# Seven half-size products in place of eight for w_out in a gated MLP with linear attention, with one centring pass and a new order of steps

## The chip, the cores and the metric

The kernel runs on one core of one Trainium2 chip. The time is the core's device time for one execution, in microseconds (us), as a median of several runs. The engines are TensorE (PE, with its weight loads as PEld), VectorE (DVE), ScalarE (ACT), GpSimd (POOL) and the queue of SyncE (SP), which issues the loads and stores. Matmuls read SBUF and add up in PSUM.

## What is computed

Eight batches of linear attention (8 heads, 576 positions, 64 channels) feed a gated MLP whose gate mixes positions. Cut to what matters:

```python
q_s = softmax(q, axis=-1); k_s = softmax(k, axis=2)      # each with 1e-9 added to the sum
kv = np.einsum('bhsd,bhse->bhde', k_s, v)
x = np.einsum('bhsd,bhde->bhse', q_s, kv)                # -> (8, 576, 512)
h = gelu_tanh(x @ w_in)                                  # w_in 512 x 1024
u, v = h[..., :512], h[..., 512:]
v_n = (v - mean(v)) / np.sqrt(var(v) + 1e-06) * g_ln     # over the 512 channels
v_s = np.einsum('ts,bsd->btd', w_sg, v_n) + b_sg[None, :, None]   # w_sg 576 x 576
out = x + (u * v_s) @ w_out                              # w_out 512 x 512
```

## The kernel before

All is float32, and every dense product is made of numbers split in two: a high part rounded to the fast matmul format and a low part that holds the rest. A product is then three matmuls, high by high, high by low and low by high, added in PSUM. The low part is made by one subtraction, the high part by one cast.

The channels of a batch lie on the 128 partitions in blocks of 128, and the 576 positions along the row in two halves of 288. A batch goes through these steps, each a small function: the softmax of q and k (`q_max`, `q_sub`, `q_exp`, `q_sum`, `q_inv`, `q_mul`, and `k_...`, with copies between partition groups in `q_swapm`, `q_swapd`, `k_rota`, `k_rotb`), `kv_mm`, `xm_mm` (x and its two parts `xm_high`, `xm_low`), `hv_mm b i` (the v half of w_in for one block of 128 positions, 12 matmuls of 512 columns), `hu_mm b f` (the u half for one block of channels, 24 matmuls of 288 columns; batch 0 has it in pieces, `hu_part`), the norm (`hv_gelu`, `hv_sq` or the statistics in `hv_stat`, `hv_pow`, `hv_norm`, `hv_high`, `hv_low`, and `tail_...` for the last 64 positions), `sg_mm b d` (the product with w_sg, 28 matmuls of 288), `gate b d` (times u), `gate_high`, `gate_low`, `out_mm b e` (w_out, 24 matmuls of 288 for each of four blocks e, 96 a batch), `out_base` (x again, from its two parts), `out_add` (PSUM added to it) and `out_store`. In the last batch the last block is done in two halves (`last_mm`, `last_add`, `last_store`).

`hv_norm` takes the mean off and multiplies by g_ln in one pass on DVE; `hv_high` and `hv_low` apply 1/sqrt(var) as a scale while they make the two parts:

```python
V.scalar_tensor_tensor(out=t, in0=t, scalar=mean, in1=g_bc[n], op0=op, op1=ALU.mult)
A.activation(vn_h()[:, i], v_s(b, i), AF.Copy, scale=rs_s(b, i))
V.scalar_tensor_tensor(out=lo[:, i], in0=v_s(b, i), scalar=rs_s(b, i), in1=f32(hi[:, i]), op0=ALU.mult, op1=ALU.subtract)
```

The order of all this is written out by hand: the string `PLAN` names the steps one after the other, a letter behind a step choosing the engine (V, A, G for DVE, ACT, POOL). Each engine runs its own steps in the order of that string; `InOrder` (its helper `issue`, line 163 of the profile, L180 afterwards) binds DVE, ACT, POOL and SP to it, and `mm` (line 252, afterwards L283) binds PE. So steps of three or four batches are interleaved: while one batch is in its gate, the next ones are in their softmax and norm. Nothing overtakes on an engine.

PSUM has eight banks. Three pairs (`ps2`, names ps_0_77, ps_1_78, ps_2_79) turn round for the products whose result has two halves of 288, one bank for each half; two single banks (`ps1`, ps_0_80, ps_1_81) turn round for hv_mm and kv_mm. A tile that is filled again waits for what still reads it. The framework keeps waits by tile: for a pair of banks, a matmul into one half counts as touching the tile that DVE reads.

At the start the weights come as 64-bit numbers, are turned into floats by integer operations (`wi_a` to `wi_d`, `wo_a` to `wo_d`) and split. `warm n` is a pair of matmuls with the identity whose result nobody reads; there are eight of them, all before the first hu_part.

## Time and profile before

| | before |
|---|---|
| median of 3 runs | 495.14 us (494.0 to 495.35) |
| the profiled execution | 495.75 us, of which span 494.0 |
| PE busy | 480.7 us, 97% |
| DVE busy | 348.5 us, 71% |
| ACT busy | 285.6 us, 58% |
| POOL busy | 168.8 us, 34% |

The span is the time from the first to the last instruction that the profiler saw; the run's own time is 1.75 us longer. Matmuls overlap, so their mean duration (298 ns for 288 columns) is not the distance from one to the next; that is read from starts. Rows of groups give the number of instructions, then their busy time and the mean in ns, then the idle time before them. Rows of a timeline give the start, the duration, the engine, the line of the code and the operation with its tiles; "f32 x4" there is a merged run of four.

### The profile page before, as it was taken

The page shows a single profiled execution, that of the slowest core. Times are in us where ns is not written, and L with a number is a line of the kernel's source. Part 1 is how long each engine was busy: PE and PEld are TensorE (multiplying, and loading weights), DVE is VectorE, ACT ScalarE, POOL GpSimd, SP SyncE. Part 2 cuts the span into 40 slices and gives each one's busy share as a digit, 9 for nine tenths or more (in the row PEclk, how much of TensorE's full clock was granted, in tenths as well). Part 3 has the DMA queues.
Part 4 walks back from the last instruction along what each step waited for, and adds up shares of the span by engine and source line. Part 5 has one row for each costly group of instructions (what it writes and reads, how often), then busy time and mean ns, then how long its engine had stood idle before and what let it go on. Part 6 is the DMA issues. An engine that isn't in the chain of part 4 may idle for free.

```text
span 494.0 us, 9497 instructions
## 1 busy us (share of the span) xinstructions
PE 480.7 (97%) x3847; PEld 445.6 (90%) x3847; DVE 348.5 (71%) x611; ACT 285.6 (58%) x607; POOL 168.8 (34%) x133
## 2 busy tenths in 40 slices
...
DMA packets 16302, 47.51 MB, mean 96 GB/s; under 512 B 1922, under 2 KB 3332, under 8 KB 16260
## 3 DMA queue, kind: packets, MB, share of 16 engines
...
## 4 chain that ended last, share of the span: by engine, by line
PE 80%; DVE 9%; DMA 3%; ACT 3%; POOL 2%; issue 2%; SPq 0%; POOLq 0%
PE ps L252 80%; DMA raw_i_vnh<-w_in 1%; DVE v L163 1%; DMA vv<-v 1%; POOL qq L163 1%; DVE ot_i L163 1%; DVE ot_o L163 1%; POOL wi_l L163 1%; DVE km L163 1%; DVE o L163 1%; DMA eye<-identity 1%; DVE vnl L163 1%; ACT L163 1%; ACT kk L163 0%; DVE qt L163 0%
## 5 line engine op out<-in xcount | busy, mean ns | idle before, releaser
L163 POOL TENSOR_TENSOR ulow<-u,gh 128x576 fp32r<-128x576 f32 x21 | 33.4, 1593 | 90.0 <-ACT gh L163 48.5
L163 POOL TENSOR_TENSOR rs<-ve,half 128x1 f32<-128x1 f32 x36 | 26.2, 734 | 96.3 <-DVE ve L163 96.3
L252 PE MATMUL ps<-gh,wo_h 128*128 128x288 f32 x256 | 56.1, 298 | 0.0
L252 PE MATMUL ps<-ulow,wo_h 128*128 128x288 f32 x256 | 55.5, 296 | 0.0
L252 PE MATMUL ps<-gh,wo_l 128*128 128x288 f32 x256 | 55.4, 295 | 0.0
L252 PE MATMUL ps<-ws_h,vnh 128*128 128x288 f32 x256 | 55.2, 297 | 0.0
L163 DVE TENSOR_TENSOR u<-ps,u 128x576 f32<-128x576 f32 x32 | 23.8, 750 | 44.1 <-PE ps L252 39.0
L252 PE MATMUL ps<-ws_h,vnl 128*128 128x288 f32 x256 | 54.9, 296 | 0.0
L252 PE MATMUL ps<-ws_l,vnh 128*128 128x288 f32 x256 | 54.9, 296 | 0.0
L163 ACT ACT_TABLE_LOAD x34 | 43.6, 1283 | 2.7 <-issue 2.0
L163 ACT CAST gh<-u 128x576 fp32r<-128x576 f32 x32 | 20.8, 669 | 41.6 <-DVE u L163 41.5
L163 POOL TENSOR_TENSOR qq<-qq,qm 128x1152 f32<-128x1152 f32 (+2 forms) x10 | 20.9, 2092 | 67.5 <-DVE qm L163 26.8
L252 PEld LDWEIGHTS ps<-ws_h,vnh 128*128 128x128 f32 x256 | 41.4, 188 | 0.8
L252 PEld LDWEIGHTS ps<-gh,wo_h 128*128 128x128 f32 x256 | 41.3, 188 | 0.9 <-DVE x_l L163 0.2
L163 ACT ACTIVATE vnh<-v,rs 128x512 fp32r<-128x512 f32 x32 | 22.9, 723 | 33.0 <-DVE v L163 18.4
L252 PEld LDWEIGHTS ps<-gh,wo_l 128*128 128x128 f32 x256 | 41.3, 188 | 0.0
L252 PEld LDWEIGHTS ps<-ulow,wo_h 128*128 128x128 f32 x256 | 41.2, 188 | 0.0
L252 PEld LDWEIGHTS ps<-ws_h,vnl 128*128 128x128 f32 x256 | 41.1, 188 | 0.0
L252 PEld LDWEIGHTS ps<-ws_l,vnh 128*128 128x128 f32 x256 | 41.0, 188 | 0.0
L252 PE MATMUL ps<-x_h,wi_h 128*128 128x288 f32 (+2 forms) x256 | 40.6, 298 | 0.4 <-DVE o L163 0.3
L163 DVE TENSOR_TENSOR o<-ps,o 128x576 f32<-128x576 f32 (+1 forms) x33 | 24.0, 729 | 23.4 <-PE ps L252 20.5
L252 PE MATMUL ps<-wi_h,x_h 128*128 128x512 f32 x144 | 39.8, 397 | 0.4 <-ACT v L163 0.4
(128 smaller groups left out, 1116.5 us busy)
## 6 DMA issues: line engine op xcount, KB each, us to landing
...
out<-o SPq DMA_DIRECT2D x31, 288.0 KB, 2.7
...
ghws<-w_sg SPq DMA_DIRECT2D x5, 288.0 KB, 8.4
x_lk<-k_turn SPq DMA_DIRECT2D x4, 288.0 KB, 4.3
...
raw_i_vnh<-w_in SPq DMA_DIRECT2D x2, 512.0 KB, 7.4
```

Of the source, the lines that this page charges most:

```text
L163: ins = op(*args, **kw)
L252: tc.keep_in_program_order(nc.tensor.matmul(*args, **kw))
```

## The change

From batch 1 on (`FROM`) w_out is done by the scheme of Strassen and Winograd. The gated u (512 channels) and w_out (512 by 512) are cut in halves of 256 channels, u also in halves of 288 positions; seven products of half size (`out_p b t m`, m from 1 to 7, t for the two blocks of 128 output channels in a half, six matmuls each) replace the eight. Their operands are quarters of u and four sums of them, made in place (`t_1` to `t_4`) and split (`p_high`, `p_low`) into three slots each; the weights' sums are made once (`s1_a` to `s4_b`, `s_h`, `s_l`). The products of a t lie in the two banks of one PSUM pair, some on top of each other, and are added to out_base in between by six additions (`o_p1`, `o_p2`, `o_u2`, `o_u4`, `o_p4`, `o_p3`), five of them of 288 columns and `o_u2` of 576. A batch has 84 matmuls there and 12 additions, where it had 96 and 4. `apart` tells the framework that a matmul into one bank of the pair and DVE's read of the other don't wait for each other.

The factor g_ln moves from the norm to `gate`, which becomes an operation with two inputs and a factor per partition; the bias rows of sg_mm are divided by it (`g_safe`, `g_rows`, twelve small copies by the SP queue). `hv_cen` centres and scales v in one pass, by DVE or by ACT; `hv_high` is then a plain cast and `hv_low` a plain subtraction, on DVE or POOL. The square in `hv_sq` is written to PSUM. q, k and v share four slots; v comes in one load; the copies of the softmax between partition groups take both halves at once (`q_swapm 3` in place of `q_swapm 3 0` and `q_swapm 3 1`). The last block's halves (`last_mm`) are gone. `PLAN` is written anew from end to end. The diff without most of it:

```diff
+NU, NH, NL, NO, NV, NM, NK = 3, 3, 3, 2, 3, 2, 4
+FROM = 1
...
+k_mb 1 1, warm 0, warm 6, load_w_in 6, wi_a 6 A, q_top 1 1, wi_b 6, k_mc 1 1, wi_c 6, hu_part 0 0 0, hu_gpart 0 0 0, q_sub 1 1 V, hu_part 0 2 1
...
+g_safe, ws_h 3 A, k_ma 2 1, hv_stat 0 4 A, hv_mm 1 3, hv_pow 0 4, ws_l 0 V, hv_cen 0 2 V, hv_gelu 1 3 A, hv_sq 1 3, g_rows, ws_l 3 V, ws_h 2 A
...
+sg_mm 7 1, hu_mm 7 3, hu_gelu 7 3, gate 7 1, gate 7 0, p_high 7 1 A, t_1 7 V, sg_mm 7 3, out_store 6 1, sg_mm 7 2, gate 7 3, out_base 7 3 G
+p_low 7 1 V, out_base 7 1 G, p_high 7 5 A, out_p 7 1 1, gate 7 2, out_base 7 2 G, p_low 7 5 G, out_base 7 0 G, t_2 7 V, p_high 7 2 A, out_p 7 0 1
+p_low 7 2 V, out_p 7 1 2, out_p 7 0 2, o_p1 7 1, p_high 7 6 A, p_low 7 6 V, out_p 7 1 6, t_3 7 V, o_p1 7 0, o_p2 7 0, p_high 7 7 A, out_p 7 0 6
+p_low 7 7 V, out_p 7 0 7, o_p2 7 1, p_high 7 3 A, p_low 7 3 G, o_u2 7 0, out_p 7 1 7, out_p 7 0 5, o_u2 7 1, out_p 7 1 5, t_4 7 G, o_u4 7 0
+out_p 7 0 3, o_u4 7 1, o_p3 7 0, out_store 7 0, out_p 7 1 3, p_high 7 4 A, p_low 7 4 V, out_p 7 0 4, o_p3 7 1, out_store 7 1, o_p4 7 0, out_store 7 2
+out_p 7 1 4, o_p4 7 1, out_store 7 3
...
     def mm(*args, **kw):
-        tc.keep_in_program_order(nc.tensor.matmul(*args, **kw))
+        ins = nc.tensor.matmul(*args, **kw)
+        tc.keep_in_program_order(ins)
+        return ins.ins
...
     def wo_hl():
-        return late("wo_h", [P, 4, DM]), late("wo_l", [P, 4, DM])
+        return late("wo_h", [P, 7, 2, HD]), late("wo_l", [P, 7, 2, HD])
...
+    PLACE = {(0, 0): 0, (1, 0): 1, (1, 1): 2, (0, 1): 6}
...
+    def s1_a(E=G):
+        hi = f32(wo_hl()[0])
+        E.tensor_tensor(out=temp(1, 0), in0=hi[:, 6], in1=hi[:, 2], op=ALU.add)
...
+    def s_h(i, E=A):
+        rounded(E, wo_hl()[0][:, 2 + i], temp(i, (i + 3) % 4))
...
-    def load_g():
-        Y.dma_start(out=g_bc, in_=g_ln.broadcast_to([P, DV]))
...
+    def load_g(E=Y):
+        E.dma_start(out=gp, in_=g_ln)
...
+    def g_safe():
+
+        V.scalar_tensor_tensor(out=gt, in0=gp, scalar=-1.0, in1=gp, op0=ALU.mult, op1=ALU.max)
+        V.tensor_scalar(out=gt, in0=gt, scalar1=2.0 ** -64, scalar2=2.0 ** -64, op0=ALU.is_lt, op1=ALU.mult)
+        V.tensor_tensor(out=gp, in0=gp, in1=gt, op=ALU.add)
+        V.reciprocal(out=gi, in_=gp)
+        V.tensor_copy(out=gi_h, in_=gi)
+        V.tensor_tensor(out=gi_l, in0=gi, in1=f32(gi_h), op=ALU.subtract)
+
+    def g_rows():
+        for row, z in ((TL, gi_h), (TL + 1, gi_l), (TL + 32, gi_h)):
+            for d in range(4):
+                Y.dma_start(out=f32(vn_2[row:row + 1, d * P:(d + 1) * P]), in_=f32(z[:, d:d + 1]))
 
...
     def load_v(b, h):
-        Y.dma_start(out=vv[h][:, 0:ST], in_=v[b, h, :, 0:ST])
-        Y.dma_start(out=vv[h][0:TL, ST], in_=v[b, h, 0:TL, ST])
+        if b > 1:
+            kq("v", b, h)
+        Y.dma_start(out=vv_s(b, h), in_=v[b, h])
...
+    def q_swapm(b, h=None):
+        swap(both(qs_s, b, h), both(qm_s, b, h))
...
-        A.activation(sq[n], v_s(b, i)[n], AF.Square, bias=nm_s(b, i)[n], accum_out=sv_s(b, i)[n])
+        A.activation(st["hv", b, i][n], v_s(b, i)[n], AF.Square, bias=nm_s(b, i)[n], accum_out=sv_s(b, i)[n])
...
-    def hv_norm(b, i):
+    def hv_cen(b, i, E=A):
 
         n = rows(b, i)
-        t = v_s(b, i)[n]
-        mean, op = (nm_s(b, i)[n], ALU.add) if (b, i) in nm_s.turn else (mv_s(b, i)[n, 0:1], ALU.subtract)
-        V.scalar_tensor_tensor(out=t, in0=t, scalar=mean, in1=g_bc[n], op0=op, op1=ALU.mult)
-
-    def hv_high(b, i):
-        A.activation(vn_h()[:, i], v_s(b, i), AF.Copy, scale=rs_s(b, i))
-
-    def hv_low(b, i):
+        t, rs, nb = v_s(b, i)[n], rs_s(b, i)[n], nb_s(b, i)[n]
+        mean, sign = (nm_s(b, i)[n], 1.0) if (b, i) in nm_s.turn else (mv_s(b, i)[n, 0:1], -1.0)
+        V.tensor_scalar(out=nb, in0=mean, scalar1=rs, scalar2=sign, op0=ALU.mult, op1=ALU.mult)
+        if E is A:
+            A.activation(t, t, AF.Identity, bias=nb, scale=rs)
+        else:
+            V.tensor_scalar(out=t, in0=t, scalar1=rs, scalar2=nb, op0=ALU.mult, op1=ALU.add)
+
+    def hv_high(b, i, E=A):
+        rounded(E, vn_h()[:, i], v_s(b, i))
+
+    def hv_low(b, i, E=V):
         hi, lo = vn_h(), vn_l()
-        V.scalar_tensor_tensor(out=lo[:, i], in0=v_s(b, i), scalar=rs_s(b, i), in1=f32(hi[:, i]), op0=ALU.mult, op1=ALU.subtract)
...
     def gate(b, d):
-        u = split(u_s(b, d))
-        V.tensor_tensor(out=u, in0=st["g", b, d][:, :, 0:HS], in1=u, op=ALU.mult)
-
-    def gate_high(b, d):
-        A.copy(out=gh_s(b, d, at=d), in_=u_s(b, d))
+        u = split(u_of(b, d))
+        V.scalar_tensor_tensor(out=u, in0=st["g", b, d][:, :, 0:HS], scalar=gp[:, d:d + 1], in1=u, op0=ALU.mult, op1=ALU.mult)
...
+    def gate_high(b, d, E=A):
+        rounded(E, parts_of(b, d)[0], u_of(b, d))
 
     def gate_low(b, d, E=V):
-        gl = u_s("low", b, d, at=8 * b + 4 + d, dt=F32R)
-        E.tensor_tensor(out=gl, in0=u_s(b, d), in1=f32(gh_s(b, d)), op=ALU.subtract)
+        hi, lo = parts_of(b, d)
+        E.tensor_tensor(out=lo, in0=u_of(b, d), in1=f32(hi), op=ALU.subtract)
+
+    FIRST, LAST = slice(0, HS), slice(HS, S)
+    TURNS = (1, 2, 5, 6, 7, 4, 3)
+
+    def quarter(b, n, cs):
+        return u_pair(b, n)[:, :, cs]
+
+    def t_1(b, E=G):
+        z = quarter(b, 0, LAST)
+        E.tensor_tensor(out=z, in0=z, in1=quarter(b, 0, FIRST), op=ALU.subtract)
+
+    def t_2(b, E=G):
+        z = quarter(b, 0, LAST)
+        E.tensor_tensor(out=z, in0=quarter(b, 1, LAST), in1=z, op=ALU.subtract)
+
+    def t_3(b, E=G):
+        z = quarter(b, 0, FIRST)
+        E.tensor_tensor(out=z, in0=quarter(b, 0, LAST), in1=z, op=ALU.subtract)
+
+    def t_4(b, E=G):
+        z = quarter(b, 1, FIRST)
+        E.tensor_tensor(out=z, in0=z, in1=quarter(b, 0, LAST), op=ALU.subtract)
+
+    def operand(b, m):
+        return quarter(b, *{1: (0, FIRST), 2: (1, FIRST), 3: (1, LAST), 4: (1, FIRST), 5: (0, LAST), 6: (0, LAST), 7: (0, FIRST)}[m])
+
+    def part(z, b, m):
+        return z(b, m, at=2 * FROM + 7 * (b - FROM) + TURNS.index(m), shape=[P, 2, HS])
+
+    def p_high(b, m, E=A):
+        rounded(E, part(hi_s, b, m), operand(b, m))
+
+    def p_low(b, m, E=V):
+        E.tensor_tensor(out=part(lo_s, b, m), in0=operand(b, m), in1=f32(part(hi_s, b, m)), op=ALU.subtract)
+
+    def out_p(b, t, m):
+        w_h, w_l = wo_hl()
+        n, ts = (0, 1, 6, 2, 3, 4, 5)[m - 1], slice(t * P, t * P + P)
+        if m == 1:
+            bank(ps2, "o", b, t)
+        to = st["o", b, t][:, 0 if m in (1, 6, 5, 3) else 1, 0:HS]
+        pairs = []
+        for c in range(2):
+            g, l = part(hi_s, b, m)[:, c], part(lo_s, b, m)[:, c]
+            pairs += [(w_h[:, n, c, ts], g), (w_h[:, n, c, ts], l), (w_l[:, n, c, ts], g)]
+        fresh = m in (1, 2, 7)
+        for i, (l, r) in enumerate(pairs):
+            apart(b, t, 0 if m in (1, 6, 5, 3) else 1, "mm", mm(to, l, r, start=fresh and i == 0, stop=i == len(pairs) - 1, skip_group_check=not fresh))
...
+    banks = {}
+
+    def apart(b, t, n, kind, ins):
+
+        log = banks.setdefault(id(st["o", b, t]), [])
+        for m, other, earlier in log:
+            if m != n and other != kind:
+                tc.declare_no_dep(ins, earlier, reason="another PSUM bank")
+        log.append((n, kind, ins))
+        del log[:-80]
+
+    def into(b, t, z, n):
+        ps = st["o", b, t]
+        ins = V.tensor_tensor(out=z, in0=ps[:, :, 0:HS] if n is None else ps[:, n, 0:HS], in1=z, op=ALU.add)
+        if n is not None:
+            apart(b, t, n, "sum", ins.ins)
+
+    def o_p1(b, t):
+        into(b, t, o_of(b, t)[:, FIRST], 0)
...
+    def o_p3(b, t):
+        into(b, t, o_of(b, t)[:, LAST], 0)
 
...
     def out_store(b, e):
-        Y.dma_start(out=out[b, e * P:(e + 1) * P, :], in_=o_s(b, e))
...
-    def last_mm(b, j):
-        if not j:
-            bank(ps2, "o", b, 3)
-        pairs = out_pairs(b, 3)
-        for m, (l, r) in enumerate(pairs):
-            mm(st["o", b, 3][:, j, 0:HS], l, r[j], start=m == 0, stop=m == len(pairs) - 1)
-
```

The order on PE shows the product stage of batch 3. Before, after the last sg_mm and hu_mm of that batch (ps_0_77) came two kv products of batch 5 (vv, kk) and then the four out_mm, 24 matmuls of one block in a row; gh and ulow are the high and low part of the gated u, wo_h and wo_l those of the weights:

```order
L252 MATMUL ps_0_77<-x_h_1923,wi_h 128x288 x8
L252 MATMUL ps_0_77<-x_h_1923,wi_l 128x288 x8
L252 MATMUL ps_0_77<-x_l_1962,wi_h 128x288 x8
L252 MATMUL ps_1_81<-vv_75,kk_1_2508 64x65 x20
L252 MATMUL ps_0_80<-vv_74,kk_0_2514 64x65 x20
L252 MATMUL ps_1_78<-gh_0_3011,wo_h 128x288 x2
L252 MATMUL ps_1_78<-ulow_0_3047,wo_h 128x288 x2
L252 MATMUL ps_1_78<-gh_0_3011,wo_l 128x288 x2
L252 MATMUL ps_1_78<-gh_1_3008,wo_h 128x288 x2
L252 MATMUL ps_1_78<-ulow_1_3052,wo_h 128x288 x2
L252 MATMUL ps_1_78<-gh_1_3008,wo_l 128x288 x2
L252 MATMUL ps_1_78<-gh_2_3056,wo_h 128x288 x2
```

After the change the same stage starts with hu_mm 3 2 (x_h, x_l), product 1 (hi_1, lo_1) of one t, one hv_mm of batch 4 (128x512) and then product 2 (hi_2, lo_2) of the same t:

```order
L283 MATMUL ps_2_79<-x_h_1951,wi_l 128x288 x8
L283 MATMUL ps_2_79<-x_l_1958,wi_h 128x288 x8
L283 MATMUL ps_0_77<-hi_1_2893,wo_h 128x288
L283 MATMUL ps_0_77<-lo_1_2895,wo_h 128x288
L283 MATMUL ps_0_77<-hi_1_2893,wo_l 128x288
L283 MATMUL ps_0_77<-hi_1_2893,wo_h 128x288
L283 MATMUL ps_0_77<-lo_1_2895,wo_h 128x288
L283 MATMUL ps_0_77<-hi_1_2893,wo_l 128x288
L283 MATMUL ps_1_81<-wi_h,x_h_2671 128x512 x4
L283 MATMUL ps_1_81<-wi_h,x_l_2673 128x512 x4
L283 MATMUL ps_1_81<-wi_l,x_h_2671 128x512 x4
L283 MATMUL ps_0_77<-hi_2_2948,wo_h 128x288
```

The blocks of 24 are cut into pieces of six, and each piece has its own operand to wait for.

Later in that stage product 7 of the second t is followed at once by product 5 of the first and then by product 5 of the second, which lies in the bank that products 6 and 7 of that t have just filled (ps_1_78):

```order
L283 MATMUL ps_1_78<-hi_7_3042,wo_h 128x288
L283 MATMUL ps_1_78<-lo_7_3047,wo_h 128x288
L283 MATMUL ps_1_78<-hi_7_3042,wo_l 128x288
L283 MATMUL ps_0_77<-hi_5_2944,wo_h 128x288
L283 MATMUL ps_0_77<-lo_5_2982,wo_h 128x288
L283 MATMUL ps_0_77<-hi_5_2944,wo_l 128x288
L283 MATMUL ps_0_77<-hi_5_2944,wo_h 128x288
L283 MATMUL ps_0_77<-lo_5_2982,wo_h 128x288
L283 MATMUL ps_0_77<-hi_5_2944,wo_l 128x288
L283 MATMUL ps_1_78<-hi_5_2944,wo_h 128x288
L283 MATMUL ps_1_78<-lo_5_2982,wo_h 128x288
```

No other work stands between them on PE.

On DVE the end of the program before was three gates (u from ps), two low parts, and five additions to o out of PSUM:

```order
L163 TENSOR_TENSOR u_2_5147<-ps_1_78,u_2_5147 128x576
L163 TENSOR_TENSOR u_1_5180<-ps_2_79,u_1_5180 128x576
L163 TENSOR_TENSOR ulow_1_5308<-u_1_5180,gh_1_5276 128x576
L163 TENSOR_TENSOR u_3_5182<-ps_0_77,u_3_5182 128x576
L163 TENSOR_TENSOR ulow_3_5317<-u_3_5182,gh_3_5315 128x576
L163 TENSOR_TENSOR o_2_5150<-ps_1_78,o_2_5150 128x576
L163 TENSOR_TENSOR o_1_5216<-ps_2_79,o_1_5216 128x576
L163 TENSOR_TENSOR o_3_5177<-ps_0_77,o_3_5177 128x288
L163 TENSOR_TENSOR o_0_5052<-ps_1_78,o_0_5052 128x576
L163 TENSOR_TENSOR o_3_5177<-ps_0_77,o_3_5177 128x288
```

Now the gates of batch 7 (with gp, the factor) are mixed with half sums of u_0 (128x2x288), low parts of the seven operands and additions of half the size; these rows are followed by some twenty more of the same kinds:

```order
L180 SCALAR_TENSOR_TENSOR u_1_5037<-ps_2_79,gp,u_1_5037 128x576
L180 TENSOR_TENSOR lo_1_5273<-u_0_5086,hi_1_5210 128x576
L180 SCALAR_TENSOR_TENSOR u_1_5037<-ps_0_77,gp,u_1_5037 128x576
L180 TENSOR_TENSOR u_0_5086<-u_1_5037,u_0_5086 128x2x288
L180 TENSOR_TENSOR lo_2_5299<-u_1_5037,hi_2_5291 128x576
L180 TENSOR_TENSOR o_1_5271<-ps_1_78,o_1_5271 128x288
L180 TENSOR_TENSOR lo_6_5316<-u_0_5086,hi_6_5314 128x576
L180 TENSOR_TENSOR u_0_5086<-u_0_5086 128x2x288
L180 TENSOR_TENSOR o_0_5285<-ps_2_79,o_0_5285 128x288 x2
L180 TENSOR_TENSOR lo_7_5335<-u_0_5086,hi_7_5327 128x576
L180 TENSOR_TENSOR o_1_5271<-ps_1_78,o_1_5271 128x288
L180 TENSOR_TENSOR o_0_5285<-ps_2_79,o_0_5285 128x576
```

What was two low parts and five additions behind the gates is now a row of low parts, sums and additions between which the seven products stand on PE.

## Rows read from the trace of the kernel before

**Rows 1.** Part 1 of the page: busy time, share and instructions by engine.
```profile
PE 480.7 (97%) x3847; PEld 445.6 (90%) x3847; DVE 348.5 (71%) x611; ACT 285.6 (58%) x607; POOL 168.8 (34%) x133
```

**Rows 2.** Waits of PE: line, releaser: us in total, times, longest.
```profile
PE ps L252 <- DMA eye<-identity: 4.4, 1, 4.4
...
PE ps L252 <- DVE o L163: 0.3, 1, 0.3
```

**Rows 3.** Stretches: length; busy PE, PEld, DVE, ACT, POOL; PE clock, DMA, GB/s.
```profile
28.20:107.60 79.40, 78.68 (x639) 70.84 (x639) 77.28 (x138) 66.52 (x154) 44.76 (x33) 1.00 0.44 158
107.60:300.00 192.40, 192.40 (x1530) 176.91 (x1531) 146.98 (x253) 116.30 (x254) 62.42 (x45) 1.00 0.26 89
300.00:490.40 190.40, 190.34 (x1492) 182.09 (x1490) 102.07 (x176) 82.34 (x163) 49.33 (x36) 1.00 0.12 43
```

**Rows 4.** Timeline of PE, two stretches: start, duration, engine, line, operation.
```profile
94.63 0.42 PE L252 MATMUL ps<-ulow,wo_h 128*128 128x288 f32 x2
...
106.80 0.42 PE L252 MATMUL ps<-gh,wo_l 128*128 128x288 f32 x2
...
301.26 1.10 PE L252 MATMUL ps<-wi_h,x_l 128*128 128x512 f32 x4
302.20 1.09 PE L252 MATMUL ps<-wi_l,x_h 128*128 128x512 f32 x4
```

**Rows 5.** Groups by line and form: count | busy, mean ns | idle before, releasers.
```profile
L163 POOL TENSOR_TENSOR ulow<-u,gh 128x576 fp32r<-128x576 f32 x21 | 33.4, 1593 | 90.0 <-ACT gh L163 48.5 <-ACT nm L163 18.9 <-DVE ulow L163 15.7
...
L163 DVE SCALAR_TENSOR_TENSOR vnl<-v,rs,vnh 128x512 fp32r<-128x512 f32 x32 | 26.2, 825 | 2.5 <-ACT vnh L163 2.4
...
L163 DVE TENSOR_TENSOR u<-ps,u 128x576 f32<-128x576 f32 x32 | 23.8, 750 | 44.1 <-PE ps L252 39.0 <-ACT u L163 5.1
L163 DVE TENSOR_TENSOR o<-ps,o 128x576 f32<-128x576 f32 x31 | 23.0, 746 | 21.8 <-PE ps L252 18.9 <-POOL o L163 2.3 <-issue 0.5
L163 ACT ACTIVATE vnh<-v,rs 128x512 fp32r<-128x512 f32 x32 | 22.9, 723 | 33.0 <-DVE v L163 18.4 <-POOL rs L163 9.8 <-DVE kr L163 4.7
...
L163 ACT CAST gh<-u 128x576 fp32r<-128x576 f32 x32 | 20.8, 669 | 41.6 <-DVE u L163 41.5
L163 DVE SCALAR_TENSOR_TENSOR v<-v,nm,g_bc 128x512 f32<-128x512 f32 x22 | 20.4, 933 | 1.0 <-ACT sq L163 1.0
...
L163 ACT ACTIVATE u<-ps 128x576 f32<-128x576 f32 x28 | 18.1, 650 | 27.3 <-PE ps L252 26.5 <-POOL ulow L163 0.7
...
L163 ACT COPY qs<-qm 32x36 f32<-32x36 f32 x56 | 12.3, 219 | 8.6 <-DVE qm L163 7.8
...
L163 DVE TENSOR_TENSOR ulow<-u,gh 128x576 fp32r<-128x576 f32 x11 | 8.8, 796 | 5.8 <-ACT gh L163 5.4 <-POOL ulow L163 0.5
...
L252 PE MATMUL ps<-eye 128*128 128x128 f32 x32 | 6.8, 384 | 4.4 <-DMA eye<-identity 4.4
...
L163 DVE TENSOR_TENSOR o<-ps,o 128x288 f32<-128x288 f32 x2 | 0.9, 458 | 1.7 <-PE ps L252 1.7
```

**Rows 6.** Timeline of 301.9 to 308.5 us: the multiplication twice, POOL's subtraction.
```profile
302.00 0.75 DVE L163 TENSOR_TENSOR qq<-qq,qd 128x576 f32<-128x576 f32 x1
...
304.48 3.33 POOL L163 TENSOR_TENSOR kk<-kk,km 128x1280 f32<-128x1280 f32 x1 [10.26 <-issue]
...
304.91 3.51 DVE L163 TENSOR_TENSOR qq<-qq,qd 128x576 f32<-128x576 f32 x1
```

**Rows 7.** Timeline of the end: the last matmul and the last addition.
```profile
490.04 0.29 PE L252 MATMUL ps<-gh,wo_l 128*128 128x288 f32 x1
490.37 0.46 DVE L163 TENSOR_TENSOR o<-ps,o 128x288 f32<-128x288 f32 x1 [0.83 <-PE ps L252]
```

**Rows 8.** DMA issues: count, KB each, median us from issue to landing.
```profile
out<-o SPq DMA_DIRECT2D x31, 288.0 KB, 2.7
...
raw_i_vnl<-w_in SPq DMA_DIRECT2D x2, 512.0 KB, 8.7
...
out<-o SPq DMA_DIRECT2D x2, 144.0 KB, 1.8
```

481 lines of the change are left out of this document (286 added, 195 removed).

## Prediction

> **What bounds the kernel now.** I read the page's busy line first [rows 1]: TensorE (PE) is busy for 480.7 us of the 494.0 us span, VectorE (DVE) for 71%, ScalarE (ACT) for 58%, GpSimd (POOL) for 34%. Busy is not the same as streaming, so I went on to what PE waits for: six waits in the whole run, 9.4 us together, the longest at the very start for the identity matrix [rows 2] (the first and the last of the six stand there). The table by stretches [rows 3] then places them. From 28.2 us, when the first dense product of the MLP starts, to 490.4 us PE is idle for 0.78 us out of 462.2, and its clock is at 2.4 GHz (granted 1.00). So nearly the whole time is PE's stream, and a matmul that goes is worth its pitch as long as the stream stays unbroken. The pitch is read from starts, since durations overlap: in the w_out products 46 pairs of 128x288 matmuls take 106.80 - 94.63 = 12.17 us, 0.132 us each; four 128x512 matmuls take 302.20 - 301.26 = 0.94 us, so one hv_mm (twelve) is 2.8 us [rows 4]. The same table shows what has room: after 107.6 us DVE is busy for 147.0 of 192.4 us and later for 102.1 of 190.4. Before that it has none: 77.3 of 79.4 us.
>
> **What goes: 84 matmuls.** A batch's w_out stage has 96 matmuls of 288 columns. With seven products it has 7 x 2 x 6 = 84, in seven batches, so 84 fewer; the order of the changed program counts no other change on PE. 84 x 0.132 = **11.1 us less**, all of it on the path, as nothing on PE hides it. The Trainium skill ("TensorE: Matmul & The Clock Gate", Back-to-back issue gap) gives a lone stream N/2.4 + 2.5 ns, 122.5 ns for 288 columns, and then 10.3 us; the pitch of rows 4 says otherwise here, where every matmul also loads its weights, and the sum goes by it.
>
> **What comes: work on the other engines.** Durations from rows 5. DVE loses 36 centring passes (0.933) and 32 low parts of the 0.825 form, 60 us. It gains 17 half sums and 16 low parts (0.796), 14 plain low parts of the norm (at most 0.796), 17 two-constant passes for centring (at most 0.933, as no row shows the form), and 39 more additions out of PSUM of 0.458 in place of 13 of 0.746 that go (70 halves and 18 whole ones for 2 and 31): 13 + 13 + 11 + 16 + 21 = 74 us. So DVE is up by some 14 us in 480 at the most. ACT gains 21 casts (0.669) and 19 centrings (0.723), 28 us, and loses 48 of the swap copies (0.219) and as many rotations, some 20. POOL gains the most, about 38 operations of the 1.593 form, net of what goes to DVE some 45 us, to 44% of the span. No engine becomes the bound on average. The factor in the gate makes 32 two-operand passes into three-operand ones: 0 to 0.17 us each, by 0.750 against 0.825, and on SP's queue sixteen loads of v's last block (none of PE's six waits is for one) are gone. **All this is nothing on the path while PE has something to do, and the price is only where PE's order has no cover.** There are three such places.
>
> **The product stage, batches 1 to 6.** In the changed order products of hv_mm and hu_mm stand between the seven. I walked batch 3 from the end of its last sg_mm (0), with 0.8 us for six matmuls and 0.2 us from PE's end to DVE's start (490.04 + 0.13 to 490.37) [rows 7]. hu_mm 3 2 (24 matmuls) ends at 3.2, product 1 at 4.0, hv_mm 4 2 at 6.8; then product 2 is due. Its operand needs the GELU 0.65, the gate 0.75, the cast 0.67 and the low part 0.80, one after the other: 3.2 + 0.2 + 2.87 = 6.3, and with handoffs 6.5. Slack 0.3 us. Products 6 and 7 have over 3 us. Product 5 of the second half must wait for the addition that reads products 6 and 7: product 7 ends at 20.8, plus 0.2 + 0.75 + 0.1 is 21.85, when PE was ready at 21.6 after product 5 of the first half: **0.25 to 0.35 us lost**. Products 3 and 4 have 0.6 us of slack. So 0.35 us a stage, 2.0 us for six; bounds 0 (the planner's order hides it) and 1.6 (one POOL operation, see the first rival), so 0 to 9.6 us.
>
> **The end, batch 7.** Nothing is left to put between the products. Same walk, 0 at the end of the last sg_mm: gate 0.75, second half sum 0.80 and low part 0.80 follow, so product 2 can start at 2.65, and PE has two product 1 (1.6 us): 1.05 lost. Then DVE has six operations in a row (0.46, 0.80, 0.80, 0.46, 0.46, 0.80) to 6.3, PE four products to 5.85: 0.5 lost before product 7. Before product 5 another 0.25. Before product 4 the third half-sum on POOL, the cast, and on DVE an addition and the low part reach 12.2, PE 11.45: 0.75. Together **2.5 us lost**. The last store is of a whole block, 288 KB, in place of a half: 2.7 against 1.8 us to landing [rows 8], 0 to 0.9, taken as 0.5. So +3.0, with bounds of 1 and 4.5.
>
> **The start.** Two of the eight warm-up groups now stand among the hu_part products. One is 6.8 us / 8 = 0.85 us of PE [rows 5], so 1.7 if PE had work to do, nothing if it waits there; 1.0 taken. Two things bound it wider. DVE, full in this stretch [rows 3], drops 5 x (0.933 + 0.825) us for batch 0 and gets 9 cheaper passes and six sums of weights: up to 1.5 us sooner. But hv_mm 0 0 now comes after seven hu_part products and not after eight and a kv product, while the weights it needs come from the same DVE queue, up to 4 us of waiting. And twelve small copies of 1/g into vn_2, which the first sg_mm reads, now stand on SP's queue behind DVE's g_safe; the three hv_mm between cover 8.4 us, and the slowest kind of weight load takes 8.7 to landing [rows 8], so this costs little and is within the same 4 us. Loads in another order move bytes, not their sum. -1.5 to +4.
>
> **Sum.** The profiled execution took 495.75 us (span 494.0 and 1.75 around it). 495.75 - 11.1 + 2.0 + 3.0 + 1.0 = 490.65; the median of the runs is 495.14, 0.6 lower, so **490 us**.
>
> **Rivals.**
> *POOL blocks DVE in every stage.* The one row that speaks most against the change: at 304.48 POOL starts a 3.33 us subtraction, and DVE's multiplication of 0.75 us, issued at 304.91, takes 3.51 and ends 0.6 after it [rows 6]. DVE with two operands in SBUF waited for the whole of POOL's operation. (The Trainium skill, "SBUF — State Buffer", Who interferes with whom, calls the pair of ports that DVE and POOL share an exclusive lock, held for the whole instruction; the row agrees.) Now POOL's half sums, low parts and bases run back to back through the product stage, and DVE's low part of product 2, slack 0.3, is such an operation. If each of the six stages loses one operation of POOL, 1.59 us, the sum is 495.1 - 11.1 + 4.0 + 9.5 = 497.5, **slower**; it decides from 1.45 us a stage on. Against it: DVE's waits of this kind occur in the kernel before too, and PE did not stop for them. 20%, four of these just within the measurement's reach.
> *Everything streams.* The order hides the stages, and DVE's relief shows at the start: 495.1 - 11.1 + 3.0 - 1.5 = 485.5. 18%.
> *The start runs late by 4 us:* 490 + 3 = 493 to 494. 12%.
> *The waits per bank are not parted:* were PE's half to wait for DVE's read of the other, some 60 of the 84 additions would cost 0.2 + 0.46 + 0.1 us, about 45 us, to 530. The program's waits stand at the first matmul of a product alone, which speaks against it: 2%.
>
> **How the numbers follow.** The forecast has 48%. A measurement of this kernel tells 0.3% from no change, that is 1.5 us: faster ends at 493.65, slower begins at 496.6. Faster: 48 + 18 + 2 of the late start = 68%. Within: 10 of the late start + 4 of the first rival = 14%. Slower: 16 + 2 = 18%. The range leaves out the parted-waits case and the upper part of the first rival: 484 to 497.5.
>
> **What would show it.** Right: PE idle within the last 14 us in pieces of 0.3 to 1 us before products 2, 7, 5 and 4; waits of PE of 0.2 to 0.4 us for DVE's o in each stage; 3300 matmul instructions against 3384 at the same pitch; POOL above 40%. Wrong: PE waits of over a microsecond for lo or hi in every batch (first rival), no PE wait after 110 us but the last stage (second), or a first dense product later than 30 us (third). The forecast falls too if the pitch of products that load new weights for every matmul is not the 0.132 us of before.

## The result and the profile after

The changed kernel takes **489.29 us** (median of 4 runs, 487.25 to 491.01), the kernel before in the same session 494.67 (494.00 to 495.35): a ratio of 0.989, 95% interval 0.985 to 0.993, so about 5.4 us faster. The forecast was 490. The profiled execution took 489.02 us with a span of 487.2, against 495.75 and 494.0 before: 6.7 us less, and this is the sum that the steps below have to make.

The busy line of the changed kernel, to lay beside [rows 1] (columns: busy us, share of the span, instructions):

```profile
PE 471.3 (97%) x3763; PEld 433.4 (89%) x3763; DVE 380.5 (78%) x681; ACT 295.5 (61%) x558; POOL 221.3 (45%) x177
```

PE has 84 matmuls fewer (3763 against 3847) and is still the engine that is always busy. Of the others only DVE took far more work than the prediction gave it: 32.0 us more where it had said 14 at the most. ACT's 9.9 and POOL's 52.5 us are near its 8 and 45.

What PE waits for, against [rows 2], without the rows that end by the first dense product (line, releaser: us in total, times, longest):

```profile
...
PE ps L283 <- DVE kt L180: 1.2, 1, 1.2
...
PE ps L283 <- DVE lo L180: 0.7, 2, 0.4
PE ps L283 <- DVE kvt L180: 0.7, 2, 0.3
PE ps L283 <- ACT x_h L180: 0.6, 2, 0.4
PE ps L283 <- DVE o L180: 0.3, 1, 0.3
...
```

The first dense product starts at 28.62 us (28.20 before). Behind it stand the one for kt at 43 us, one each of kvt and x_h at 58, one for o at 149.5, and the two for lo, which are the end. The old kernel had two behind its first dense product:

```profile
67.80 1.21 PE L252 MATMUL ps<-wi_h,x_h 128*128 128x512 f32 x4 [0.38 <-ACT v L163]
...
107.56 1.33 PE L252 MATMUL ps<-x_h,wi_h 128*128 128x288 f32 x8 [0.34 <-DVE o L163]
```

From start to start, against the pitch of the same shape, these two holes are 0.65 and 0.60 us long (the matmul behind a hole takes 0.1 us more as well, here and below), and the changed kernel has neither.

The stretches answer those of [rows 3] (length; busy PE, PEld, DVE, ACT, POOL; PE clock, DMA share, GB/s):

```profile
28.00:62.00 34.00, 32.11 (x273) 26.88 (x274) 33.67 (x67) 30.75 (x67) 14.16 (x12) 1.00 0.54 206
62.00:150.00 88.00, 87.54 (x666) 81.66 (x665) 82.82 (x136) 60.73 (x124) 60.71 (x46) 1.00 0.21 69
150.00:300.00 150.00, 149.94 (x1228) 137.71 (x1227) 119.97 (x221) 94.77 (x174) 67.27 (x52) 1.00 0.30 101
300.00:470.00 170.00, 170.00 (x1336) 161.19 (x1335) 110.41 (x196) 84.50 (x152) 64.17 (x50) 1.00 0.16 52
470.00:483.30 13.30, 12.50 (x87) 11.45 (x85) 10.24 (x18) 3.37 (x5) 2.82 (x2) 1.00 0.08 30
```

Two stretches lose time: the first, with 1.9 us of idle PE and DVE full, and the last 13 us, with 0.8. A stretch's idle time counts only what lies between the matmuls' modelled ends. From start to start, against the pitch of the same shape, the holes are a little longer: 2.4 us in the first and 1.9 in the last. From 62 to 470 us PE is idle for 0.52 of 408 us, though from 150 to 470 us DVE works 230 us and POOL 131.

The start, PE alone (start, duration, engine, line, operation; in brackets the idle time before and what ended it):

```profile
41.08 0.75 PE L283 MATMUL ps<-x_l,wi_h 128*128 128x320 f32 x4
42.98 0.43 PE L283 MATMUL ps<-eye,kt 128*128 128x128 f32 x2 [1.15 <-DVE kt L180]
43.17 1.18 PE L283 MATMUL ps<-wi_h,x_h 128*128 128x512 f32 x4
...
57.46 0.53 PE L283 MATMUL ps<-x_h,minus 128*128 128x288 f32 x2 [0.18 <-ACT x_h L180]
58.31 1.20 PE L283 MATMUL ps<-qt,kvt 64*64 64x288 f32 x16 [0.33 <-DVE kvt L180]
```

Four matmuls of 320 columns take 0.59 us from start to start, so at 41.08 PE has work until 41.67, and 1.31 us pass to 42.98. The first product of hv_mm (wi_h,x_h) then starts at 43.17. In the kernel before it starts at 43.40, almost the same time, but by then that kernel had done one hu_part product and one kv product more, and none of the two warm-up groups that now stand there.

And the end, against [rows 7]: of PE's starts in the last stage the matmul ahead of the first large hole, the two that waited and the last one, with the last addition:

```profile
472.02 0.40 PE L283 MATMUL ps<-hi,wo_h 128*128 128x288 f32 x1
472.81 0.40 PE L283 MATMUL ps<-lo,wo_h 128*128 128x288 f32 x1 [0.40 <-DVE lo L180]
...
481.86 0.40 PE L283 MATMUL ps<-lo,wo_h 128*128 128x288 f32 x1 [0.28 <-DVE lo L180]
...
483.30 0.29 PE L283 MATMUL ps<-hi,wo_l 128*128 128x288 f32 x1
483.63 0.46 DVE L180 TENSOR_TENSOR o<-ps,o 128x288 f32<-128x288 f32 x1 [0.34 <-PE ps L283]
```

The second matmul of product 2 starts 0.79 us after the first where 0.13 is the pitch, and 0.66 are lost; the second of the last product's first half likewise, 0.44.

### The profile page after: what moved, and what is told of

The parts are those of the page before. It is cut to its first block, busy times and chain, and to the rows that moved or that the text cites. A ratio compares the mean times of both kernels' runs of the same rounds, so it can differ in the third digit from the quotient of the medians.

```text
span 487.2 us, 9417 instructions
## 1 busy us (share of the span) xinstructions
PE 471.3 (97%) x3763; PEld 433.4 (89%) x3763; DVE 380.5 (78%) x681; ACT 295.5 (61%) x558; POOL 221.3 (45%) x177
## 4 chain that ended last, share of the span: by engine, by line
PE 77%; DVE 13%; DMA 6%; issue 2%; ACT 1%; SPq 1%; POOL 1%; DVEq 0%; ACTq 0%
PE ps L283 77%; DMA raw_i_wo_h<-v 2%; DVE ot_o L180 1%; DVE qd L180 1%; DVE km L180 1%; DMA kqq<-q 1%; DMA raw_i_wo_l<-w_in 1%; DMA x_lk<-k_turn 1%; DVE u L180 1%; DVE o L180 1%; DVE kqq L180 1%; DVE ot_i L180 1%; DVE qm L180 1%; DVE x_l L180 1%; DVE qt L180 1%
## 5 line engine op out<-in xcount | busy, mean ns | idle before, releaser
L180 ACT CAST hi<-u 128x576 fp32r<-128x576 f32 x51 | 33.9, 670 | 61.2 <-DVE u L180 38.2
L283 PE MATMUL ps<-hi,wo_h 128*128 128x288 f32 x212 | 62.0, 298 | 0.5 <-DVE o L180 0.3
L283 PE MATMUL ps<-lo,wo_h 128*128 128x288 f32 x212 | 61.6, 297 | 0.7 <-DVE lo L180 0.7
L180 DVE TENSOR_TENSOR o<-ps,o 128x288 f32<-128x288 f32 (+1 forms) x88 | 44.1, 512 | 22.1 <-PE ps L283 21.0
L283 PE MATMUL ps<-hi,wo_l 128*128 128x288 f32 x212 | 61.2, 295 | 0.0
L180 POOL TENSOR_TENSOR lo<-u,hi 128x576 fp32r<-128x576 f32 x24 | 36.4, 1523 | 44.9 <-ACT hi L180 44.7
L283 PEld LDWEIGHTS ps<-hi,wo_h 128*128 128x128 f32 x212 | 39.4, 188 | 2.5 <-DVE o L180 1.1
L283 PEld LDWEIGHTS ps<-lo,wo_h 128*128 128x128 f32 x212 | 39.4, 188 | 2.0 <-DVE lo L180 1.1
L283 PE MATMUL ps<-x_h,wi_l 128*128 128x288 f32 (+2 forms) x256 | 39.8, 295 | 0.0
L283 PE MATMUL ps<-x_l,wi_h 128*128 128x288 f32 (+2 forms) x256 | 39.7, 295 | 0.0
```

The lines of the kernel that those rows point to most:

```text
L180: ins = op(*args, **kw)
L283: ins = nc.tensor.matmul(*args, **kw)
```

## The experiments

The changed kernel's 489.29 us comes from four runs (487.25 to 491.01), and the kernel before read 494.68 to 495.19 in the sessions of the experiments. A difference of under some 2 us from the changed kernel is therefore read from the traces and not from the medians.

**Is a matmul of the products worth its pitch, and is there slack?** The first product of each half is computed twice, 84 matmuls more, as many as the change took away. The operand has long been there, so nothing else is asked of any engine.

```
+        for again in range(2 if m == 1 else 1):
             for i, (l, r) in enumerate(pairs):
                 ...
```

> Each first product (two a batch, six matmuls of 288 columns each) is done twice from batch 1 on; the second time writes the same sums again. That is 84 matmuls more, as many as the change took away. Theory stream (PE's stream sets the time, a matmul that goes is worth its pitch of 0.1325 us): 84 x 0.1325 = 11.1 us more than the changed kernel, less what the two repeats of the last batch cover: PE waits there 0.23 and 0.66 us at the start of the second product, which the 1.6 us of repeats fill. So +10 to +11 us, about 499.5 us. Rival slack (the waits between the products are so many that repeats fall into them): +8 us or less, under 497.5 us.

Measured: 501.49 us (499.78 to 502.50), ratio to the kernel before 1.0135, interval 1.0106 to 1.0165; 12.2 us above the changed kernel, where 10 to 11 had been expected. The 84 matmuls cost at least their 11.1 us, so the stream theory holds and the slack that the rival needed isn't there. The profiled executions are 13.2 us apart: 11.1 for the matmuls, 3.1 for holes behind 110 us (8.0 in place of 4.9, from start to start), less 1.1 for a start that came sooner. Two of the holes that opened stand in the first stage of products (batch 1), and ahead of them DVE worked beside POOL:

```profile
133.97 1.45 POOL L180 TENSOR_TENSOR lo<-u,hi 128x576 fp32r<-128x576 f32 x1 [0.39 <-ACT hi L180]
134.05 1.99 DVE L180 TENSOR_TENSOR km<-km 128x256 f32<-128x256 f32 x2
...
139.84 0.40 PE L283 MATMUL ps<-hi,wo_h 128*128 128x288 f32 x1 [0.80 <-ACT hi L180]
140.71 0.40 PE L283 MATMUL ps<-lo,wo_h 128*128 128x288 f32 x1 [0.47 <-DVE lo L180]
```

In the changed kernel POOL's low part comes later, and the two operations on k take 0.75 us:

```profile
134.12 0.75 DVE L180 TENSOR_TENSOR km<-km 128x256 f32<-128x256 f32 x2
```

Its product starts at 139.92. In this execution PE was ready 1.0 us sooner, DVE's gate came 0.9 later (138.28 against 137.42), and PE waited: there the operands, not PE, set when the product starts.

**Do the waits have to be kept apart by bank?** Without that bookkeeping, PE's write to one half of the pair of banks waits for DVE's read of the other.

```
-            if m != n and other != kind:
-                tc.declare_no_dep(ins, earlier, reason="another PSUM bank")
+            pass
```

> The changed kernel without the note that the two banks of a pair don't wait for each other. Prediction's price of parted waits: some 60 of the 84 additions cost PE 0.2 + 0.46 + 0.1 us, about +45 us, 534 us, if products and additions of the two banks follow each other that closely everywhere. Rival order (the written order already puts other work between an addition of one bank and the next product into the other, so only the last batch and two or three places of each stage pay): +5 to +15 us, 494 to 504 us. Rival nothing (the framework's waits never bind): within 1 us of 489.

Measured: 497.02 us (496.81 to 497.26), ratio 1.0046, interval 1.0025 to 1.0066; 7.9 us above the changed kernel. PE now waits for o eight times, 4.4 us, in place of once (and for 0.84 us at 146.74, put down to an operation of ACT that writes to PSUM). The longest of the eight:

```profile
343.52 0.40 PE L283 MATMUL ps<-hi,wo_h 128*128 128x288 f32 x1 [0.91 <-DVE o L180]
```

From start to start PE's holes behind 110 us grow by 7.7 us, from 4.9 to 12.7, so they are the whole difference. The waits by bank are worth 7.9 us, more than the whole gain: without them the change is slower than the old kernel. But the 45 us that the prediction's last rival put on it are wrong by a factor of six. It charged 60 additions with a wait each; the order puts something else between most products and the additions that read them.

**What does the start wait for?** Three edits there. First the two warm-up groups among the hu_part products are taken out.

```
-k_mb 1 1, warm 0, warm 6, load_w_in 6, ...
+k_mb 1 1, load_w_in 6, ...
```

> The two warm-up groups among the first hu_part products are left out (nobody reads them). Theory weights (the first hv_mm starts when ACT has cast the last block of w_in, at 43.0 us, and PE has a hole of 1.3 us ahead of it anyway): the hole grows by 0.9 us, the first hv_mm still starts at 43.1 to 43.3 us, and the time stays at 489 +- 0.4. Rival busy (PE's own stream sets the start, as the prediction took it): 0.9 us less, 488.4 us, and the first hv_mm at 42.2 to 42.4 us.

Measured: 489.01 us (488.46 to 489.27), ratio 0.9885: no change against the changed kernel. The hole ahead of kt grew from 1.31 to 1.75 us (from start to start), and one of 0.40 opened ahead of km at 36.73; together that is nearly the 0.9 us that the warm-ups had filled:

```profile
39.94 0.76 PE L283 MATMUL ps<-x_l,wi_h 128*128 128x320 f32 x4
42.28 0.43 PE L283 MATMUL ps<-eye,kt 128*128 128x128 f32 x2 [1.59 <-DVE kt L180]
42.47 1.18 PE L283 MATMUL ps<-wi_h,x_h 128*128 128x512 f32 x4
```

In both executions the first hv_mm comes 14.55 us after the first dense product (28.62 to 43.17; 27.92 to 42.47). PE's own work between them doesn't set it. The two groups are free where they stand.

Second, a product of the next batch that PE does later (kv_mm 1 0, with its load and its scaling) is put into the hole, where the old kernel had one; the second product of that kind (kv_mm 1 1) moves forward too, ahead of the first x products. Cut to the first of the two:

```
-wi_h 7 A, wi_l 4 V, k_top 1 1, wi_l 6 G, hu_part 0 3 1, ...
+wi_h 7 A, wi_l 4 V, load_v 1 0, k_top 1 1, kv_mm 1 0, kv_inv 1 0, kv_scale 1 0, wi_l 6 G, hu_part 0 3 1, ...
```

> In the start the first kv product of batch 1 (1.3 us of PE) is moved from behind the first two hv_mm to ahead of the last hu_part, with its load and its two small DVE steps, so that it stands in the hole before the first hv_mm; the second kv product of batch 1 is moved ahead of the x products of the first half, so that its DVE steps lie beside them. Theory order (the start lost time because PE had nothing ready while the last weights were converted, and work that is ready fills the hole): first hv_mm at 43.2 to 43.7 us as before, and behind it PE 0.9 us sooner, and 0.4 to 0.5 us more where the second kv product waited: 1.0 to 1.5 us less, 488 us. Rival DVE (DVE is full until 77 us and sets the pace there, so PE meets the same waits later): holes of the same sum appear before 77 us, time within 0.4 us of the changed kernel.

Measured: 489.09 us (488.74 to 490.88), ratio 0.9895: no change again, where the theory had said 1.0 to 1.5 us less. The hole at 43 us is filled, hv_mm starts at 43.06, and the time comes back 10 to 15 us later:

```profile
PE ps L283 <- ACT x_h L180: 1.5, 1, 1.5
PE ps L283 <- ACT kqk L180: 0.5, 1, 0.5
...
```

(waits of PE from 40 to 62 us). PE's order isn't what holds the start. DVE's kvt, for which PE waits at 58, comes at 57.97 in the changed kernel and at 58.10 here. The third edit leaves PE alone and has DVE do the row maxima of q (q_max) of batch 1 twice, at about 23 and 32 us. By the starts of the operations behind them each doubling adds 1.39 us, 2.8 together, a little more than the 2.5 expected.

```
-... q_max 1 0, load_w_in 4, ...
+... q_max 1 0, q_max 1 0, load_w_in 4, ...
...
-wi_l 5 G, q_max 1 1, ...
+wi_l 5 G, q_max 1 1, q_max 1 1, ...
```

> DVE's two maxima of q of batch 1, at 23 and 32 us, are each done twice (2 x 1.27 = 2.5 us of DVE, the same result). Theory pace (DVE, busy for 116 of the 121 us from 28.5 to 150 us, sets the pace of the first 150 us through PE's holes at 43, 57, 77 and 149 us): all of it appears, +2.0 to +2.7 us, 491.5 us. Rival stream (PE's holes there are single waits that have room beside them): under +0.8 us.

Measured: 492.67 us (10 runs, 491.43 to 493.63), ratio 0.9959, interval 0.9946 to 0.9971; 3.4 us above the changed kernel.

```profile
29.54 0.69 PE L283 MATMUL ps<-eye,km 128*128 128x128 f32 x2 [2.06 <-DVE km L180]
45.90 0.32 PE L283 MATMUL ps<-eye,kt 128*128 128x128 f32 x1 [1.59 <-DVE kt L180]
```

kt, a DVE result, frees PE at 45.90 in place of 42.98, 2.9 later. DVE sets the pace there, and its time goes into the end time in full. This execution also has a later wait (1.6 us for a load of v) that the changed kernel doesn't show. Whether ACT has room there was not run. It is busy for 30.75 of the 34 us, and its last cast of wi_h, which hv_mm reads, ends as late as kt:

```profile
41.87 1.12 ACT L180 CAST wi_h<-ot_i 128x512 fp32r<-128x512 f32 x2
```

**Has DVE room later?** The same doubling in batches 4 to 7, eight times (the first is shown), 11 us of DVE in a stretch where it is busy for 230 of 320 us.

```
-... q_max 4 0, hu_mm 2 1, ...
+... q_max 4 0, q_max 4 0, hu_mm 2 1, ...
...
```

> The same maxima are done twice in batches 4, 5, 6 and 7 (eight more, 10 us of DVE between 165 and 420 us, same result), none in batch 1. Theory pace (from 150 us on DVE has 30% room and PE streams): +0.0 to +0.6 us, 489 to 490 us, though four times as much work as in the early twin. Rival even (DVE's added work costs wherever it is): +2 us or more.

Measured: 494.79 us (10 runs, 493.38 to 497.12), ratio 1.0003, interval 0.9984 to 1.0022; 5.5 us above the changed kernel. My theory had said 0 to 0.6: it fell. Half of the inserted time is on the path, and PE's holes behind 110 us, from start to start, grow by 5.4 us. Two of the waits:

```profile
235.00 0.53 PE L283 MATMUL ps<-ws_h,vnh 128*128 128x288 f32 x2 [1.30 <-DVE x_l L180]
...
271.89 0.40 PE L283 MATMUL ps<-hi,wo_h 128*128 128x288 f32 x1 [1.19 <-DVE o L180]
```

Each batch got 2.8 us. Behind the doublings of batches 4, 5 and 7 PE waited for 1.06, 1.30 and 1.32 us, each time for x_l, which stands behind them in DVE's queue, and in two of the three for ACT's u as well; behind those of batch 6 not at all. So the written order hides one to two microseconds of DVE at three of these places, and not the quarter of free time that the busy share suggests: what runs behind an inserted operation in DVE's queue is late by it until the next gap. The wait at 271.89 is another case: it lies 39 us behind the nearest doubling ahead of it, DVE stood idle for 0.37 us just before, and its cause is open.

**What does the end cost?** First, batch 7 is multiplied as a whole as in the old kernel, 12 matmuls more and no half sums. One quarter of w_out has been overwritten by a sum by then and is used as it is, so the last batch's output is not the reference's; shapes and counts are as they would be.

```
-... out_p 7 1 1, ... out_p 7 0 6, ... o_p4 7 1, out_store 7 3
+... gate_low 7 3 V, out_base 7 3 G, out_base 7 0 G, out_mm 7 2, out_add 7 2
+out_mm 7 1, out_store 7 2, out_add 7 1, last_mm 7 0, ... last_add 7 1, out_store 7 0, last_store 7 1
```

> Batch 7 alone goes back to four whole products of w_out with 96 matmuls, the last block in two halves as in the kernel before; batches 1 to 6 keep the seven products. Theory end (the seven products of the last batch save 12 x 0.1325 = 1.6 us of PE and lose 1.9 us in waits at the second, sixth/fifth and last products, since nothing is left to put between them): the waits go, the matmuls come, the stretch from the last sg_mm's end to the end of the span goes from 17.0 us to 16.6 to 16.8, time 0 to 0.5 us less. Rival whole products wait as well (their operands pass the same gate, cast and subtraction): the stretch grows by up to 1.6 us.

Measured: 487.72 us (487.01 to 488.28), ratio 0.9865, interval 0.9847 to 0.9883; 1.6 us below the changed kernel by the medians, but the intervals overlap. The last stage itself tells more. From the last sg_mm start to the end of the span the changed kernel takes 17.19 us, and four other runs with the same last stage (no warm-ups between, kv in the hole, more DVE late, tiles at 64 bytes) 17.20 to 17.24; here it is 16.44. PE has no wait for lo, and 0.3 of the 0.75 us are on PE, so there the twelve matmuls (1.6 us) cost a little less than the waits that they replace. The other 0.4 lie behind the last matmul. A form that keeps the original quarter needs 4 KB more of a partition and was not run.

Second, a cheaper cure of the same waits: inside each product the matmuls that read the low part come last.

```
-            g, l = part(hi_s, b, m)[:, c], part(lo_s, b, m)[:, c]
-            pairs += [(w_h[:, n, c, ts], g), (w_h[:, n, c, ts], l), (w_l[:, n, c, ts], g)]
+            g = part(hi_s, b, m)[:, c]
+            pairs += [(w_h[:, n, c, ts], g), (w_l[:, n, c, ts], g)]
+        for c in range(2):
+            pairs += [(w_h[:, n, c, ts], part(lo_s, b, m)[:, c])]
```

> In each of the seven products the two matmuls that read the low part stand at the end of the six and not second and fifth. Theory end (PE's waits in the last batch are for the low part at the second matmul of a product: 0.66 at the second product and 0.44 at the last): three more matmuls, 0.4 us, come ahead of it, so these two shrink by 0.4 each; 0.8 us less, 488.4 us, and the other waits stay. Rival chain (the waits behind a product only move to the next one, since DVE's row of sums and low parts is what ends last there): the last matmul ends as before, 489.2 us.

Measured: 487.91 us (487.49 to 489.48), ratio 0.9876, interval 0.9853 to 0.9899; 1.4 us below the changed kernel by the medians, 0.7 by the profiled executions (span 486.5). The stretch from the last sg_mm start is 16.50 us, 0.7 less than in the five runs above, where 0.8 had been expected.

```profile
472.26 0.29 PE L283 MATMUL ps<-hi,wo_l 128*128 128x288 f32 x1
...
472.52 0.29 PE L283 MATMUL ps<-hi,wo_l 128*128 128x288 f32 x1
472.82 0.53 PE L283 MATMUL ps<-lo,wo_h 128*128 128x288 f32 x2
```

The low part still arrives at 472.8, but PE has done three more matmuls by then, and 0.16 us are lost in place of 0.66. Of the versions that compute all of the reference this one has the lowest median; its interval overlaps the changed kernel's.

**Why are unchanged matmuls quicker?** The holes and terms so far sum to 5.4 us of gain (next section) where the profile has 6.7. The rest is in rows that the change doesn't touch. A stage of sg_mm has 112 matmuls with the same operands in both kernels; its first start and the next product's first start, before and after:

```profile
462.47 0.43 PE L252 MATMUL ps<-ws_h,vnh 128*128 128x288 f32 x2
...
477.40 0.43 PE L252 MATMUL ps<-gh,wo_h 128*128 128x288 f32 x2
```

```profile
232.16 0.43 PE L283 MATMUL ps<-ws_h,vnh 128*128 128x288 f32 x2
...
246.98 0.43 PE L283 MATMUL ps<-x_h,wi_h 128*128 128x288 f32 x2
```

14.93 us before, 14.82 after, with no wait in either: 133.3 and 132.3 ns apiece. What differs is where the allocator put the operands, and what the other engines do meanwhile. So the old kernel got a tile of 32 bytes that shifts the norm's parts and all later tiles.

```
     half = sb("half", [P, 1])
+    shift = sb("shift", [P, 8])
+    G.memset(shift, 0.0)
```

> The kernel before with one more tile of 32 bytes a partition ahead of the norm's tiles, so that all later tiles lie 32 bytes further: the norm's parts vnh, vnl and vn come to a multiple of 64 bytes (as in the kernel after), of the two buffers of x's parts the ones of odd batches come to such a place and those of even batches leave it; the instructions and their order stay. Place theory (the unchanged matmuls are quicker in the kernel after because of where the operands lie): the starts of ws_h,vnh and ws_h,vnl matmuls go from 133.8 and 133.0 ns apart to 132.3, the ones of the two small operands vn from 134.3 to 132.4, the rows of x get quicker in odd batches and slower in even ones; 896 matmuls of the sg stage at 1 ns: about 0.8 us less, 493.5 to 494.5 in place of about 495. Rival (what the other engines do at that time sets it): all pitches stay within 0.2 ns, the time is unchanged.

Measured: 493.27 us (10 runs, 492.66 to 494.46) against 495.03 (13 runs, 493.93 to 496.35) of the kernel before beside it: ratio 0.9967, interval 0.9954 to 0.9980. The same stage:

```profile
460.11 0.42 PE L254 MATMUL ps<-ws_h,vnh 128*128 128x288 f32 x2
...
474.89 0.43 PE L254 MATMUL ps<-gh,wo_h 128*128 128x288 f32 x2
```

14.78 us, 132.0 ns apiece. But for the one fill of the new tile, same instructions, same order, other addresses: 1.8 us less, more than twice what was expected. The mean pitch of each dense row, times its count, gives 1.75 us: 0.87 in sg_mm, as expected, and 0.66 in the 512-column rows, which the expectation had left out. So the place theory holds in the old kernel. The same sum for the changed kernel's rows against the old ones is 1.8 us, and in three other runs of it (no warm-ups between, kv in the hole, low parts last) 1.75 to 1.79. The second run asked what about the place it is, with all large tiles of the changed kernel at multiples of 64 bytes (tiles of 512 bytes or more go to a pool of their own, rounded up).

```
+class Sorted:
...
+        if n < 128:
+            return self.small.tile(shape, dt, **kw)
+        t = self.large.tile([shape[0], -(-n // 16) * 16], dt, **kw)[:, 0:n]
```

> The kernel after with every tile of 512 bytes a partition or more placed at a multiple of 64 bytes (small tiles get a pool of their own behind them); in the kernel after the parts of x lie so in one of the two buffers each. Place theory: the rows of x stop alternating between batches (now 230.9 and 232.1 ns for the wi_h,x_l matmuls of 512 columns), all at the lower, and the ws,vn rows stay; some 1500 matmuls by 0.5 to 1 ns, 0.7 to 1.5 us less: 487.5 to 488.5. Rival (other engines set the pitch): the alternation stays, 489 as before.

Measured: 489.34 us (489.02 to 490.43), ratio 0.9886: no change against the changed kernel, where 0.7 to 1.5 us less had been expected. The rows moved, but these not to the lower value:

```profile
231.83 0.42 PE L299 MATMUL ps<-ws_h,vnh 128*128 128x288 f32 x2
...
246.76 0.42 PE L299 MATMUL ps<-x_h,wi_h 128*128 128x288 f32 x2
```

14.93 us, the old kernel's pitch, though by the order of the tiles in the code these operands lie at multiples of 64 bytes as in the changed kernel. The matmuls of 512 columns with wi_l got quicker (by starts, a mean of 228 ns in place of 232). By rows, the 512-column ones give 0.9 us back and sg_mm takes 0.9 more: two moves that cancel. That place matters is shown; that a multiple of 64 is what matters is refuted, and which relation of the addresses it is stays open.

## Why the prediction was right, point by point

The direction and the size were right, and so was the reason: PE's stream sets the time, and the matmuls that go are worth their pitch. That the total came out 1.6 us from the profiled execution (490.65 against 489.02) is in part luck: the start was put 1.9 too low, the stages and the end 1.1 too high each, and 1.3 us of gain were left out.

**The 84 matmuls, -11.1.** Right. The pitch in the new products is 132 to 134 ns by starts (six matmuls from 482.63 to 483.30, five steps, 0.134), and putting 84 back cost 12.2 us. The page counts 3763 matmuls in place of 3847; the forecast's 3300 and 3384 stand in no row, but their difference is right.

**The stages, +2.0.** Too high: 0.9. The walk of batch 3 was right at its place and size: product 5 of the second half starts late by 0.33 us at 268.71. But I had walked one batch and multiplied by six. In batches 2, 4, 5 and 6 the order has other work there, and PE streams, so the forecast's sign of a wait for o in each stage came in two stages only. In batch 1 the loss has another cause, and there it is 0.57 us (start, duration, engine, operation):

```profile
146.28 3.52 POOL L180 TENSOR_TENSOR kqq<-kqq,qd 128x576 f32<-128x576 f32 x2
146.87 1.92 DVE L180 TENSOR_TENSOR kqk<-kqk,km 128x1280 f32<-128x1280 f32 x1
148.71 1.41 DVE L180 TENSOR_TENSOR o<-ps,o 128x576 f32<-128x576 f32 x2
149.51 0.40 PE L283 MATMUL ps<-hi,wo_h 128*128 128x288 f32 x1 [0.31 <-DVE o L180]
```

DVE's subtraction before the addition took 1.92 us beside POOL's multiplications; alone the same form takes 1.49. That is the first rival's mechanism, in small.

**The end, +3.0.** Too high: 1.9. The waits before products 2, 5 and 4 came as walked: 0.89, 0.32 and 0.55 us against 1.05, 0.25 and 0.75. The one before product 7 (0.5) is 0.10. The last store, charged with 0.5 for its size, shows no cost between the two kernels: from the last matmul's start to the span's end it is 3.9 us in both. In the run with the last batch whole, which again ends with a half store, it is 3.5, so what the size costs stays open within 0.4.

**The start, +1.0.** Too low: about 2.9, the largest error of the sum. The changed kernel has holes of 2.4 us up to 62 us (from start to start) and of 0.4 at 77, the two warm-ups with 0.9, without which the holes would be that much longer (shown by taking them out), and a first dense product that is 0.4 later, though that differs by as much between executions of one kernel; against these stand the old kernel's two holes, 1.2, which are gone. The prediction named the mechanism and gave it up to 4 us, then took 1.0. What it misread is the cover. It set the seven hu_part products that remain against the weights of hv_mm as if PE would be the later one. In [rows 3] DVE is busy for 77.28 of the first 79.40 us; by that row DVE is as full as PE there, and with a product less on PE and none less on DVE, DVE comes last. The relief that it gave DVE in batch 0 doesn't show there: in the table above DVE is busy for 33.67 of the 34 us from 28 to 62. The three edits of the start show it from three sides. Its price for a warm-up group, 0.85 us, was too high among the products: the two groups take 0.91 together. This was the third rival, which had 12%. Its mechanism came at three quarters of its price, without its sign, since the first dense product starts at 28.62 and not later than 30, and its total of 493 to 494 was missed because the other terms were smaller too.

**What was not in the sum, -1.3.** -11.1 + 2.9 + 0.9 + 1.9 makes -5.4; measured is -6.7. What the sum leaves out is two rows: over some 2780 dense matmuls the pitch gives 1.8 us, 0.6 ns each, and the x products (matmuls of 64 columns with qt and kvt) take 0.5 us more. Nothing in the trace of before could have told the first, and the shifted old kernel says that place alone can bring as much.

**The rivals.** *POOL blocks DVE* was the one that I feared most. The block itself is there, in the changed kernel too:

```profile
311.22 2.97 POOL L180 TENSOR_TENSOR kqk<-kqk,km 128x1280 f32<-128x1280 f32 x1 [3.65 <-DVE km L180]
312.21 2.60 DVE L180 TENSOR_TENSOR lo<-u,hi 128x576 fp32r<-128x576 f32 x1 [1.06 <-ACT hi L180]
```

A low part of 0.75 us takes 2.60 and ends 0.6 us after POOL's, as in [rows 6]. Six low parts of products are stretched like this, by 0.4 to 1.9 us; counted over all of DVE's operations the time lost so is 27.6 us, and 23.9 in the old kernel (what an operation takes above the median of its form, where that is over 0.15 us; POOL is at work beside every one of them). PE waits for none of the six: the first is at 196 us, and PE's list has no wait between 149.51 and 472.81. The mechanism was right, the price was not, since the operand is made that much ahead. Where it isn't, the block does reach PE: in batch 1 above, and in the run with the first products twice, with 0.80 and 0.47 us. *Everything streams* was right for the middle and wrong at both ends. *The waits are not parted* did not happen, and would have cost 7.9 us, not 45.

**DVE's sum.** It grew by 32 us, not by 14 at the most. Left out were 36 small operations for the centring's second constant (7.3 us by the groups of the changed kernel), five subtractions of k that moved there from POOL (8.9), and six additions that make the sums of weights (4.1). The 39 more additions that the prediction names are 68 by its own brackets (70 for 2), and with these its 21 us come out. I had called all this free while PE has something to do. The late doubling of q_max prices that: at three of four places it held with one to two microseconds to spare.
